# A retention-attention and SwiGLU kernel: grouped layout, fp32 row loads on the hardware queues, casts and transposes on chip, warm-up matmuls

## The chip, the cores and the metric

The kernel runs on 1 core of a Trainium2 chip. The metric is device time in microseconds (us) of one execution. Engines are named as in the profile: PE (TensorE matmul), PEld (its weight loads), DVE (VectorE), ACT (ScalarE), POOL (GpSimd), SP (SyncE). SP, ACT and POOL also issue DMAs; the queue of the DMAs that one of them issues is called its ring here.

## The reference, cut to what matters

```python
# q, k, v: [4, 8, 768, 64] fp32; lam: [8]; D[i,j] = lam**(i-j) for i >= j
for b in range(nb):                                  # sequential over blocks
    intra = einsum(einsum(qb, kb) * Dmask, vb)
    inter = einsum(qb * lam_pow, kv_state)
    out[:, :, sl] = intra + inter
    kv_state = lam_block * kv_state + einsum(kb * rev_pow, vb)
x = out.transpose(0, 2, 1, 3).reshape(3072, 512)
y = (silu(x @ w_gate) * (x @ w_val)) @ w_out         # d_ff = 1536, y: [3072, 512] fp32
```

Both kernels use blocks of 128 tokens and bf16 matmuls. A token tile of the second half ("FFN") is 512 tokens: 12 gate/value pairs of eight 128x512 matmuls, then four output groups of twelve.

## The kernel before

It walks batch by batch and two heads at a time. Loads and stores, which the argument is about:

```python
# q, k: fp32 in memory, cast to bf16 by the software queue; v: fp32, hardware queue
for h2 in range(2):
    nc.gpsimd.dma_start(out=q_nat[:, :, h2, :], in_=q_5d[b, hp, h2])   # 128-byte rows land
    nc.gpsimd.dma_start(out=k_nat[:, :, h2, :], in_=k_5d[b, hp, h2])
    nc.sync.dma_start(out=v_raw[:, :, h2, :], in_=v_5d[b, hp, h2])     # 256-byte rows
...
nc.gpsimd.dma_start(out=wg_sb, in_=moe_w_gate.rearrange("(c p) f -> p c f", p=128))  # whole weights
nc.gpsimd.dma_start(out=wv_sb, in_=moe_w_val.rearrange("(c p) f -> p c f", p=128))
...
nc.tensor.transpose(tpq[:, blk, :], q_nat[:, blk, :, :], identity)     # all transposes on PE
...
nc.scalar.copy(out=osb, in_=op)
nc.sync.dma_start(out=out[t0:t0 + TSUB, :], in_=osb)    # a store: 128 rows of 2,048 bytes
```

## Time and profile before

| | before |
|---|---|
| time, median of 4 runs | 298.97 us |
| profiled span | 295.9 us |
| first FFN gate on ACT | 56.2 us |
| period of FFN tiles 1 to 4 | 40.1, 42.2, 41.4, 39.2 us |
| last matmul to the end | 3.6 us |

The tile rows of this and later tables are read from the instruction records: a tile starts where ACT begins the first silu of that tile.

The first lines of the page of before: span, and busy tenths in 40 slices of 7.4 us (PEclk is the clock that PE was granted, in tenths of full speed); then the packets and the chain of waits that ended last.

```profile
span 295.9 us, 4660 instructions
PE   0233614999999999999999999999999999999995
PEclk9999999999999999999999999999999999999999
DMA  9999999999999110990001000100100000001012
DMA packets 81383, 23.90 MB, mean 81 GB/s; under 512 B 75729, under 2 KB 77265, under 8 KB 81361
PE 82%; DMA 13%; POOL 1%; DVE 1%; issue 1%; ACT 0%; SPq 0%; ACTq 0%; DVEq 0%; POOLq 0%
```

The first seven slices (52 us) are an opening in which PE is mostly idle and DMA is full. From the eighth slice on PE is busy in nine tenths of every slice but the last, and its clock is full.

The DMA issues of the same page: tiles, queue, count, size, median us from issue to landing.

```profile
v_raw<-in_v_dram SPq DMA_DIRECT2D x32, 192.0 KB, 9.4
out_dram<-osb SPq DMA_DIRECT2D x24, 256.0 KB, 2.0
wg_sb<-in_moe_w_gate_dram POOLq DMA_DIRECT2D x1, 1536.0 KB, 17.1
wv_sb<-in_moe_w_val_dram POOLq DMA_DIRECT2D x1, 1536.0 KB, 24.5
```

A store of 256 KB lands in 2.0 us. In the packet records each store ends in sixteen 4-byte packets, one for each DMA engine that took part.

### The profile page before, as it was taken

The page shows a single profiled execution, that of the slowest core. Times are in us where ns is not written, and L with a number is a line of the kernel's source. Part 1 is how long each engine was busy: PE and PEld are TensorE (multiplying, and loading weights), DVE is VectorE, ACT ScalarE, POOL GpSimd, SP SyncE. Part 2 cuts the span into 40 slices and gives each one's busy share as a digit, 9 for nine tenths or more (in the row PEclk, how much of TensorE's full clock was granted, in tenths as well). Part 3 has the DMA queues.
Part 4 walks back from the last instruction along what each step waited for, and adds up shares of the span by engine and source line. Part 5 has one row for each costly group of instructions (what it writes and reads, how often), then busy time and mean ns, then how long its engine had stood idle before and what let it go on. Part 6 is the DMA issues. An engine that isn't in the chain of part 4 may idle for free.

```text
span 295.9 us, 4660 instructions
## 1 busy us (share of the span) xinstructions
PE 256.3 (87%) x1824; PEld 119.3 (40%) x1824; DVE 127.2 (43%) x296; ACT 96.6 (33%) x232; POOL 57.0 (19%) x78
## 2 busy tenths in 40 slices
PE   0233614999999999999999999999999999999995
PEld 0122302446444444464444445544444444444442
DVE  1662525477654533934453444345344433222200
ACT  3411201536342422263333224524322332222321
POOL 9765015453156000840000000000000000000000
PEclk9999999999999999999999999999999999999999
DMA  9999999999999110990001000100100000001012
GB/s 153 169 169 189 209 189 157 172 182 194 168 128 115 37 39 35 73 124 35 2 35 38 34 5 35 39 0 35 38 15 23 35 35 8 29 37 38 35 72 106
DMA packets 81383, 23.90 MB, mean 81 GB/s; under 512 B 75729, under 2 KB 77265, under 8 KB 81361
## 3 DMA queue, kind: packets, MB, share of 16 engines
q0 software_dynamic: 52816, 11.02, 41.8%
q1 hardware_dynamic: 28544, 12.59, 19.9%
q8 instruction: 14, 0.23, 0.3%
q14 instruction: 9, 0.07, 0.1%
HBM read 28.32 MB, written 6.29 MB: 117 GB/s over the span
## 4 chain that ended last, share of the span: by engine, by line
PE 82%; DMA 13%; POOL 1%; DVE 1%; issue 1%; ACT 0%; SPq 0%; ACTq 0%; DVEq 0%; POOLq 0%
PE gp L255 24%; PE vp L261 22%; PE ffn_op L272 22%; DMA v_raw<-in_v_dram 8%; PE op L225 3%; DMA q_nat<-in_q_dram 3%; PE sp L196 3%; PE op L217 3%; DMA k_nat<-in_k_dram 2%; PE tpq L171 2%; PE tpk L177 1%; PE up L232 1%; DVE ssb L204 1%; PE sp L198 1%; DVE v_s L163 0%
## 5 line engine op out<-in xcount | busy, mean ns | idle before, releaser
L263 DVE TENSOR_TENSOR h_sb<-sil,vp 128x512 bf16<-128x512 bf16 x72 | 49.5, 687 | 83.7 <-PE vp L261 81.1
L272 PE MATMUL ffn_op<-wo_sb,h_sb 128*128 128x512 bf16 x288 | 65.4, 379 | 0.2
L258 ACT ACTIVATE sil<-gp 128x512 bf16<-128x512 f32 x72 | 43.0, 598 | 60.6 <-PE gp L255 60.2
L204 DVE TENSOR_TENSOR ssb<-sp,maskp_all 128x512 bf16<-128x512 f32 x48 | 33.0, 686 | 32.5 <-PE sp L198 32.5
L261 PEld LDWEIGHTS <-wv_sb 128*128 128x128 bf16 x288 | 28.0, 98 | 35.0 <-issue 3.1
L272 PEld LDWEIGHTS <-h_sb 128*128 128x128 bf16 x288 | 27.7, 98 | 31.9 <-issue 0.2
L99 POOL DMA_DIRECT2D k_nat<-in_k_dram x32 | 26.4, 830 | 52.6 <-PE up L234 24.6
L275 ACT COPY osb<-ffn_op 128x512 f32<-128x512 f32 x24 | 14.1, 586 | 62.7 <-PE ffn_op L272 62.7
L255 PEld LDWEIGHTS <-wg_sb 128*128 128x128 bf16 x288 | 23.5, 98 | 22.9 <-issue 0.3
L98 POOL DMA_DIRECT2D q_nat<-in_q_dram x32 | 26.6, 833 | 18.8 <-DMA wg_sb<-in_moe_w_gate_dram 7.3
L255 PE MATMUL gp<-xT_285,wg_sb 128*128 128x512 bf16 x72 | 28.1, 390 | 0.0
L255 PE MATMUL gp<-xT_286,wg_sb 128*128 128x512 bf16 x72 | 27.6, 383 | 0.0
L255 PE MATMUL gp<-xT_287,wg_sb 128*128 128x512 bf16 x72 | 27.6, 383 | 0.0
L255 PE MATMUL gp<-xT_288,wg_sb 128*128 128x512 bf16 x72 | 27.6, 383 | 0.0
L261 PE MATMUL vp<-xT_285,wv_sb 128*128 128x512 bf16 x72 | 27.5, 382 | 0.0
L261 PE MATMUL vp<-xT_286,wv_sb 128*128 128x512 bf16 x72 | 27.5, 382 | 0.0
L261 PE MATMUL vp<-xT_287,wv_sb 128*128 128x512 bf16 x72 | 27.3, 379 | 0.0
L261 PE MATMUL vp<-xT_288,wv_sb 128*128 128x512 bf16 x72 | 27.3, 379 | 0.0
L171 PE MATMUL tpq<-identity,q_nat 128*128 128x128 bf16 x96 | 9.2, 240 | 20.1 <-DMA q_nat<-in_q_dram 20.1
L225 PE MATMUL op<-ssb,v_s 128*64 128x128 bf16 x96 | 15.0, 241 | 12.4 <-DVE ssb L204 12.4
L178 ACT COPY kT<-tpk 128x768 bf16<-128x768 bf16 x16 | 12.8, 799 | 23.2 <-PE tpk L177 23.0
L198 PE MATMUL sp<-qT,kT 64*128 64x128 bf16 x96 | 16.4, 237 | 0.0
(90 smaller groups left out, 264.2 us busy)
## 6 DMA issues: line engine op xcount, KB each, us to landing
v_raw<-in_v_dram SPq DMA_DIRECT2D x32, 192.0 KB, 9.4
out_dram<-osb SPq DMA_DIRECT2D x24, 256.0 KB, 2.0
q_nat<-in_q_dram POOLq DMA_DIRECT2D x32, 96.0 KB, 9.5
k_nat<-in_k_dram POOLq DMA_DIRECT2D x32, 96.0 KB, 9.7
wg_sb<-in_moe_w_gate_dram POOLq DMA_DIRECT2D x1, 1536.0 KB, 17.1
wv_sb<-in_moe_w_val_dram POOLq DMA_DIRECT2D x1, 1536.0 KB, 24.5
wo_sb<-in_moe_w_out_dram POOLq DMA_DIRECT2D x1, 1536.0 KB, 18.5
lam_bcast<-in_lam_dram POOLq DMA_DIRECT2D x1, 4.0 KB, 4.1
```

What stands on the lines that cost most here:

```text
L98: nc.gpsimd.dma_start(out=q_nat[:, :, h2, :], in_=q_5d[b, hp, h2])
L99: nc.gpsimd.dma_start(out=k_nat[:, :, h2, :], in_=k_5d[b, hp, h2])
L171: nc.tensor.transpose(tpq[:, blk, :], q_nat[:, blk, :, :], identity)
L198: nc.tensor.matmul(sp[:, 1, cs], st["kT"][64:128, bs], st["qT"][64:128, bs], start=True, stop=True)
L204: nc.vector.tensor_tensor(out=ssb, in0=sp_ap, in1=mp_ap, op=ALU.mult)
L225: nc.tensor.matmul(op[0:64, :], st["v_s"][:, blk, 0, :], ssb[:, 0, ci, :], start=False, stop=True)
L255: nc.tensor.matmul(gp, wg_sb[:, mc, fs], xT[mc][:, ts], start=(mc == 0), stop=(mc == MCHUNKS - 1))
L258: nc.scalar.activation(sil, gp, AF.Silu)
L261: nc.tensor.matmul(vp, wv_sb[:, mc, fs], xT[mc][:, ts], start=(mc == 0), stop=(mc == MCHUNKS - 1))
L263: nc.vector.tensor_tensor(out=h_sb[:, fc, :], in0=sil, in1=vp, op=ALU.mult)
L272: nc.tensor.matmul(op, h_sb[:, fc, sub * TSUB:(sub + 1) * TSUB], wo_sb[:, fc, :], start=(fc == 0), stop=(fc == FCHUNKS - 1))
L275: nc.scalar.copy(out=osb, in_=op)
```

## The change

The kernel was rewritten so that PE gets work early and attention uses the array better. A group is one block of 128 tokens of two batches, with all 8 heads; there are 12 groups. Tokens 2m and 2m+1 share a partition, so that a loaded row of q, k or v is 512 contiguous bytes. Scores, values and state updates run as 64x64 quadrants of the array, four at a time. Weights come in pieces, in order of use. Groups 0 to 3 are transposed on PE, 4 to 11 by DMA. The core of it, with cuts marked:

```diff
+    def load_fp32(g, eng, src, what, b2):          # one half: 64 partitions x 8 heads x 512 bytes
+        eng.dma_start(out=st[(what, g)][b2 * M:b2 * M + M],
+                      in_=gsrc(src, g, b2, 0, [[S * D, H], [1, 2 * D]]))
+    halves = (nc.sync, nc.scalar)                  # opening: one half on each ring
+    ...
+    def w_piece(c0, c1):                           # gate and value weights for chunks c0 to c1
+        nc.gpsimd.dma_start(out=wg_sb[:, :, cs], in_=wg_d[:, :, cs])
+        nc.gpsimd.dma_start(out=wv_sb[:, :, cs], in_=wv_d[:, :, cs])
+    ...
+    def cast_scaled(g):                            # groups 4 to 11
+        nc.scalar.copy(out=t[:, 0]..., in_=st[("kraw", g)]...)
+        nc.vector.tensor_tensor(out=t[:, 1]..., in0=st[("qraw", g)]..., in1=bap(qd, ...), op=ALU.mult)
+        nc.sync.dma_start(out=tt..., in_=t..., transpose=True)
+    ...
+    nc.tensor.matmul(sp[(c, h2)][b2 * M:b2 * M + M, n:n + BLK],       # one quadrant
+                     tt[dp, 0, s, hp, b2 * M:b2 * M + M], tt[dp, 1, :, hp, b2 * M:b2 * M + M], ...)
+    ...
+    eng.dma_start(out=bass.AP(tensor=out.tensor, offset=out.offset + row * DM + c0,
+                              ap=[[DM, 2], [2 * DM, M], [1, c1 - c0]]),   # 2 x 64 rows
+                  in_=osb[:, c0:c1])
-    nc.sync.dma_start(out=out[t0:t0 + TSUB, :], in_=osb)
+    warm_up(16) ... warm_up(10)                    # matmuls on zeros in the opening
```

The store follows from the layout: partitions 0 to 63 hold the even tokens, 64 to 127 the odd ones, so the memory side of a store has the dimensions 2, 64 and 512.

## The prediction

> **What bounds the kernel now.** The span is 295.9 us; runs take 299.5, so 3.5 us lie outside it. In the chain of waits PE is 82%, DMA 13%. The slices show two stages:
>
> 1. Opening, 0 to 52 us: PE 10 to 40% busy, the DMA rows full. 81,383 packets carry 23.9 MB, 75,729 of them under 512 B: q and k come by software queue as 128-byte rows, v as 256-byte rows. Median 9.5 us to land, wg 17, wv 24. In the chain v_raw, q_nat and k_nat hold 13% (39 us).
> 2. From 57 us PE is 9 tenths busy. In the timeline a gate/value pair of eight 128x512 matmuls takes 1.74 us start to start, an output of twelve 2.6 us: 72 x 1.74 + 24 x 2.6 = 188 us, which no layout changes. The attention block between two pairs costs 0.84 us; 48 make 40 us, 192 transposes come on top. The tail after the last matmul is 3.5 us.
>
> **What the change does.**
> - Removes the 128-byte rows: q, k, v come as 512-byte fp32 rows on the SP and ACT queues. Bytes read stay at 28 MB, packets fall to about 50,000. PE starts on the first 1 MB (k, q), FFN tile 0 before all weights, which come in pieces in order of use.
> - Adds ACT/DVE casts (128x1024, estimated 1.1 to 1.3 us from v_s 128x768 at 0.95 and kT at 0.80), v scaling on POOL (estimated 2.3 us, from the Trainium skill, "GPSIMD Engine Reference", section 3.1, tensor_tensor 4,497 ns at [128, 2048]; the trace of before has none), state copies on POOL, DMA transposes for groups 4 to 11.
> - Moves attention to 64x64 quadrants: 32 score, 8 state, 32 value, 32 update matmuls per group. In the trace a concurrent pair goes every 65 to 80 ns; I estimate a quad at 80 to 100 ns, a group at 3.1 us: 12 groups, 37 us.
> - Writes output as 2 x 64 x 512. The Trainium skill, "DMA: Bandwidth & Descriptors", section "Why a DMA increments its semaphore by 16 and not by 1", says the slowest dim sets the number of DMA engines: here 2, not 16. A 2,048-byte packet takes 78 ns in the trace, so 64 per engine are 5 us, where the last five outputs come every 2.6 us: a backlog, a tail of 12 to 14 us in place of 3.5.
>
> **Sum.** Opening until the steady loop of tile 0 (third gate/value pair) 33 us, held by POOL's order (state copies before weight pieces) and the first transpose-mask chain; rest of tile 0 28; tiles 1 to 4 37.8 each (20.9 + 10.4 + 2 x 3.1 + small stalls); tile 5 31; last outputs 10.4; tail 12. Span 265, with some chance of a short tail: time 265 us, range 250 to 281. Faster by over 2%: 0.95; within 2%: 0.04; slower: 0.01. Most of the gain is the opening.
>
> **What would show it.** PE above 9 tenths from slice 6 or 7 on; the first full-width gate matmul near 33 us; a tile period near 38 us; a group's 104 matmuls taking 3 us; out_dram landing in 5 us or more, not 2.0, and over 8 us between last matmul and end.
>
> **What would make it wrong.** Output writes over 16 engines (10 us better). Quadrants that don't run together: a group at 5 us (20 us worse). Weight pieces or ACT's own DMA issues stalling tile 0 (10 us worse). DMA transposes landing late, stalling every tile. An opening under 25 us.

The marked cut takes out a time for one store packet that stands in no trace. The packets meant are those of 2,048 bytes: they take 86 ns in the trace of before (median) and 84 ns in that of after, so 64 of them are 5.4 to 5.5 us.

## The result, and the profile after

The changed kernel is correct and slower: 321.29 us median of 4 runs, against 298.97 us. The ratio is 1.0756, with a 95% interval of 1.0708 to 1.0804. A ratio here is the mean time of one kernel's fast runs over that of the other's of the same rounds, so it isn't quite the ratio of the two medians. ("Slow" on one core only means over 1.5% above the fastest run of the same kernel.)

The same lines of the page of after; a slice is 8.0 us.

```profile
span 320.5 us, 5135 instructions
PE   6187879689606979997619996808999999999400
PEclk9669959959855997999958999976999999999955
DMA  7996999999999962749670998990940101011111
DMA packets 67064, 34.40 MB, mean 107 GB/s; under 512 B 20322, under 2 KB 64098, under 8 KB 67042
PE 31%; DMA 25%; SPq 6%; ACT 1%; issue 1%; DVE 1%; ACTq 1%; POOL 0%
DMA qkt<-qk 18%; PE bank L378 12%; PE bank L368 9%; PE bank L361 8%; DMA v<-in_v_dram 7%; SPq L90 6%; PE bank L278 1%; ACTq L386 1%; ACT osb L385 1%; DVE ssb L285 1%; ACT sil L365 1%; DVE h L371 0%; SPq L205 0%; PE bank L310 0%; PE bank L300 0%
```

The opening is short: PE is busy from the third slice on, 16 us in (some of it warm-up). But three holes follow in the PE row, at 88, 160 and 208 us, the granted clock falls to 5 to 7 tenths in or just after each, and the last slices have almost no PE work. The chain names what PE waited for: `qkt<-qk`, the DMA transposes, 18% of the span, and then loads of v (7%) and SP's own issuing of row loads (6%). None of the three is in e1's chain to more than 4%, where the stores are spread.

PE's waits in after (engine, line, releaser; us in total, times, longest), then some of PE's instructions in order of time around the first hole (start, us, what, idle time before it and its releaser). L278 are the scores, which read the transposed `qkt`; L239 the transposes on PE; L361 and L368 gate and value.

```profile
PE bank L278 <- DMA qkt<-qk: 32.0, 4, 10.2
PE bank L239 <- ACT qk L223: 8.6, 1, 8.6
```

```profile
82.05 1.03 PE L368 MATMUL bank<-xt,wv_sb 128*128 128x512 bf16 x4
...
88.02 0.73 PE L330 MATMUL bank<-v_s,qk 64*64 64x64 bf16 x32
98.37 1.07 PE L278 MATMUL bank<-qkt 64*64 64x128 bf16 x32 [9.62 <-DMA qkt<-qk]
...
101.05 1.91 PE L368 MATMUL bank<-xt,wv_sb 128*128 128x512 bf16 x4
```

PE stands still for 9.62 us before the scores of group 5. (This hole is hardly the stores' doing, as e1 shows below.) The four matmuls that took 1.03 us before it take 1.91 us after it. The Trainium skill, "TensorE: Matmul & The Clock Gate", Part 1, says that PE goes to half of its clock after an idle window of about 3.4 us. This trace agrees: the granted clock of the stretch from 68 to 122 us is 0.78.

The end of the same trace, ACT and its queue:

```profile
297.55 0.58 ACT L385 COPY osb<-bank 128x512 f32<-128x512 f32 x1 [2.00 <-PE bank L378]
298.17 2.03 ACTq L386 DMA_DIRECT2D out_dram<-osb  x1
300.30 0.37 ACT L385 COPY osb<-bank 128x256 f32<-128x256 f32 x1 [2.16 <-PE bank L378]
300.70 6.09 ACTq L386 DMA_DIRECT2D out_dram<-osb  x1
```

Issuing the last store on ACT takes 6.09 us, where a usual issue takes 0.52. The span ends at 320.5 us, 20.4 us after the last matmul. In the packet records a store ends in two 4-byte packets, and its 2,048-byte packets take 84 ns each: two DMA engines carry it, 64 packets each, 5.4 us of their time.

Where the time went, by stage (us, one profiled run each). Rows e1 to e11 are the experiments below.

| kernel | first gate | tile 0 | tile 1 | tile 2 | tile 3 | tile 4 | last matmul | tail | span |
|---|---|---|---|---|---|---|---|---|---|
| before | 56.2 | 31.5 | 40.1 | 42.2 | 41.4 | 39.2 | 292.3 | 3.6 | 295.9 |
| after | 32.1 | 36.3 | 58.3 | 48.7 | 50.7 | 33.8 | 300.1 | 20.4 | 320.5 |
| e1 | 30.9 | 36.6 | 54.4 | 35.4 | 36.7 | 34.3 | 268.0 | 4.8 | 272.7 |
| e2 | 33.1 | 38.0 | 46.4 | 33.7 | 37.4 | 34.7 | 263.5 | 20.4 | 283.8 |
| e3 | 31.3 | 37.2 | 43.7 | 38.0 | 38.0 | 35.2 | 263.0 | 4.8 | 267.8 |
| e4 | 55.8 | 32.2 | 40.1 | 42.2 | 41.4 | 39.2 | 292.6 | 19.9 | 312.5 |
| e6 | 32.2 | 37.6 | 40.9 | 35.5 | 35.4 | 34.3 | 255.6 | 4.9 | 260.5 |
| e9 | 31.8 | 35.2 | 48.6 | 36.0 | 35.4 | 34.3 | 260.8 | 4.8 | 265.6 |
| e11 | 29.8 | 37.5 | 41.3 | 35.4 | 35.4 | 34.3 | 253.2 | 4.9 | 258.1 |

(In after and in e1 to e3 and e6 to e11, "first gate" is the first full-width one: four half-width pairs come earlier, so tile 0 has ten full pairs.)

### The profile page after: what moved, and what is told of

It reads as the page before. It is cut to its first block, busy times and chain, and to the rows that moved or that the text cites. A ratio compares the mean times of both kernels' runs of the same rounds, so it can differ in the third digit from the quotient of the medians.

```text
span 320.5 us, 5135 instructions
## 1 busy us (share of the span) xinstructions
PE 237.4 (74%) x2112; PEld 117.4 (37%) x2138; DVE 105.6 (33%) x185; ACT 89.7 (28%) x149; POOL 66.9 (21%) x106
## 2 busy tenths in 40 slices
DMA packets 67064, 34.40 MB, mean 107 GB/s; under 512 B 20322, under 2 KB 64098, under 8 KB 67042
## 4 chain that ended last, share of the span: by engine, by line
PE 31%; DMA 25%; SPq 6%; ACT 1%; issue 1%; DVE 1%; ACTq 1%; POOL 0%
DMA qkt<-qk 18%; PE bank L378 12%; PE bank L368 9%; PE bank L361 8%; DMA v<-in_v_dram 7%; SPq L90 6%; PE bank L278 1%; ACTq L386 1%; ACT osb L385 1%; DVE ssb L285 1%; ACT sil L365 1%; DVE h L371 0%; SPq L205 0%; PE bank L310 0%; PE bank L300 0%
## 5 line engine op out<-in xcount | busy, mean ns | idle before, releaser
L371 DVE TENSOR_TENSOR h<-sil,bank 128x512 bf16<-128x512 bf16 (+1 forms) x74 | 49.6, 672 | 123.7 <-PE bank L368 61.7
L361 PE MATMUL bank<-xt,wg_sb 128*128 128x512 bf16 (+1 forms) x277 | 77.9, 395 | 5.9 <-DMA wg_sb<-in_moe_w_gate_dram 2.7
L368 PE MATMUL bank<-xt,wv_sb 128*128 128x512 bf16 (+1 forms) x295 | 79.8, 396 | 1.4 <-DMA wv_sb<-in_moe_w_val_dram 1.2
L365 ACT ACTIVATE sil<-bank 128x512 bf16<-128x512 f32 (+1 forms) x74 | 43.1, 585 | 107.4 <-PE bank L361 95.1
L378 PE MATMUL bank<-wo_sb,h 128*128 128x512 bf16 x283 | 66.2, 383 | 5.0 <-DVE ssb L285 4.7
L368 PEld LDWEIGHTS <-wv_sb 128*128 128x128 bf16 x296 | 30.1, 103 | 40.0 <-issue 7.8
L378 PEld LDWEIGHTS <-h 128*128 128x128 bf16 x288 | 28.7, 100 | 40.9 <-issue 8.6
L361 PEld LDWEIGHTS <-wg_sb 128*128 128x128 bf16 x296 | 28.8, 101 | 38.9 <-issue 7.1
L285 DVE TENSOR_TENSOR ssb<-bank,mask 128x512 bf16<-128x512 f32 x48 | 31.4, 683 | 32.8 <-PE bank L278 32.8
L344 POOL CAST kvz<-kvf 64x256 bf16<-64x256 f32 x40 | 15.8, 396 | 113.6 <-DVE kvf L341 110.3
L278 PE MATMUL bank<-qkt 64*64 64x128 bf16 x384 | 9.4, 249 | 33.8 <-DMA qkt<-qk 32.0
L385 ACT COPY osb<-bank 128x512 f32<-128x512 f32 (+1 forms) x24 | 13.8, 576 | 65.0 <-PE bank L378 65.0
L189 POOL TENSOR_TENSOR v_s<-v,rev 128x1024 bf16<-128x1024 f32 x12 | 23.1, 1925 | 30.8 <-DMA v<-in_v_dram 30.6
L278 PEld LDWEIGHTS <-qkt 64*64 64x64 bf16 x384 | 7.4, 125 | 35.4 <-DMA qkt<-qk 32.5
L239 PE MATMUL bank<-ident,qk 128*128 128x128 bf16 x64 | 5.2, 243 | 9.9 <-ACT qk L223 8.6
L239 PEld LDWEIGHTS <-qk 128*128 128x128 bf16 x64 | 4.5, 110 | 11.1 <-ACT qk L223 9.1
```

The costliest lines, as they stand in the source:

```text
L189: eng.tensor_tensor(out=st[("vs", g)][:, h0:h1], in0=st[("v", g)][:, h0:h1].rearrange("p h (s d) -> p h s d", s=2), in1=bap(rev, [[2, h1 - ...
L278: nc.tensor.matmul(sp[(c, h2)][b2 * M:b2 * M + M, n:n + BLK], tt[dp, 0, s, hp, b2 * M:b2 * M + M], tt[dp, 1, :, hp, b2 * M:b2 * M + M], st ...
L285: nc.vector.tensor_tensor(out=ssb[:, h2, 2 * c:2 * c + 2].rearrange("p a s n -> p (a s n)"), in0=sp[(c, h2)], in1=mask[:, h2, 2 * c:2 * c ...
L344: nc.gpsimd.tensor_copy(out=kvz[b][dp, :, h2, :], in_=kvf[b][dp])
L361: nc.tensor.matmul(gp[:, 0:N], wg_sb[:, mc, fs], xt[:, mc, b0:b1].rearrange("p b n -> p (b n)"), start=(mc == 0), stop=(mc == MC - 1))
L365: nc.scalar.activation(sil[:, 0:N], gp[:, 0:N], AF.Silu)
```

## The experiments

My theory, A: stores on two DMA engines hold up what shares those engines, the DMA transposes above all. Rival B: DMA transposes are slow by themselves, or because they stand behind row loads on SP. Rival C, later: it isn't the number of engines, but the size or count of the stores.

### e1, e2, e3, e4: stores and transposes apart

e1 splits each store in two halves of 64 partitions, one of even and one of odd rows:

```diff
-            eng.dma_start(out=bass.AP(..., offset=out.offset + row * DM + c0,
-                                      ap=[[DM, 2], [2 * DM, M], [1, c1 - c0]]), in_=osb[:, c0:c1])
+            for s in range(2):
+                eng.dma_start(out=bass.AP(..., offset=out.offset + (row + s) * DM + c0,
+                                          ap=[[2 * DM, M], [1, c1 - c0]]),
+                              in_=osb[s * M:s * M + M, c0:c1])
```

> The changed kernel with one edit: each output store is split in two of 64 partitions, so that the slowest dimension is 64 and 16 DMA engines carry it, not 2. Theory A (stores on 2 DMA engines hold up everything else on those engines, the DMA transposes above all): the transposes of groups 4 to 11 land in about 5 us, PE's waits for them (32 us) fall under 5 us, the tail after the last matmul falls from 23 us to 4 us, and the time is 255 to 265 us. Rival B (the DMA transposes are slow by themselves, or because they stand behind the row loads on the SP queue): only the tail goes, about 19 us, and the time is 300 to 305 us with the waits for the transposes still there.

e2 leaves the stores and puts all transposes on PE (groups 4 and 5, in tile 1, likewise; cut here):

```diff
-                    at(6, cast_scaled, 2 * t + 4)
-                    at(11, cast_scaled, 2 * t + 5)
+                    at(6, cast_qk, 2 * t + 4)
+                    at(7, pe_transpose, 2 * t + 4)
+                    at(11, cast_qk, 2 * t + 5)      # its pe_transpose: step 1 of the next tile
```

> The changed kernel with groups 4 to 11 cast and transposed on the chip's TensorE, as groups 0 to 3 are; the stores stay on 2 DMA engines. Theory A: no wait for a DMA transpose is left, but the stores still crowd two engines, so loads may come late and the tail stays near 15 to 23 us: 272 to 285 us. Rival B (transposes alone are to blame): the same 272 to 285 us, and then e1 gives 300 us or more. The two runs together tell them apart.

e3 is both edits.

> Both edits: stores on 16 DMA engines and all transposes on TensorE. Theory A: near e1, within 3 us, 255 to 265 us, since with free engines the DMA transposes cost PE nothing. Rival B: at least 30 us faster than e1.

e4 is the kernel before with the store's shape alone (rows land in the wrong order):

```diff
-            nc.sync.dma_start(out=out[t0:t0 + TSUB, :], in_=osb)
+            nc.sync.dma_start(out=bass.AP(..., ap=[[DM, 2], [2 * DM, 64], [1, DM]]), in_=osb)
```

> The kernel before, with its output rows written as 2 x 64 rows (even rows, odd rows), so that 2 DMA engines carry a store; the rows land in the wrong order, a wrong result on purpose. Theory A: this part of the change alone costs the tail, as four stores of 5 us come every 2.5 us at the end: 8 to 13 us more than before, 307 to 312 us, and little in the middle, where no DMA transpose waits. Rival B (store shape harmless apart from some latency): within 2% of before.

Measured (median us, ratio to before of the same rounds):

| | DMA transposes | PE transposes |
|---|---|---|
| stores on 2 engines | 321.29 (1.0756, the changed kernel) | 286.06 (0.9599, e2) |
| stores on 16 engines | 273.64 (0.9193, e1) | 268.58 (0.9014, e3) |

e4: 314.41 us, ratio 1.0555.

Splitting the stores alone takes 47.7 us off (321.29 to 273.64). Moving the transposes alone takes 35.2 us off, both together 52.7. The two don't add: stores on two engines cost 17.5 us where there are no DMA transposes, and 47.7 us where there are. The 17.5 us are nearly all tail: e2's tail is 20.4 us and e3's 4.8. e4 says the same on the other kernel: the periods of its tiles 1 to 4 are those of before to 0.1 us, its tail is 19.9 us and not 3.6, and the time is 16.3 us longer. The other 30 us arise only where DMA transposes and stores meet.

Of e1's expectations, the tail and the direction came true. The time missed the expected 255 to 265 us, because tile 1 still takes 54.4 us, and one wait for a transpose is left:

```profile
PE bank L278 <- DMA qkt<-qk: 8.3, 1, 8.3
```

That wait is again the one for group 5, the hole shown at 88 us in after: 9.62 us there, 8.27 here. In neither run does a store packet start while that transpose moves, so the stores' part in this wait is at most the 1.35 us between the two (e9 takes it up). What the split removed are the other three of after's four waits, 22.4 of the 32.0 us: 2.29 for group 6, 9.98 for group 8, 10.16 for group 10. The last two in after's chain (start, us, what), from the issue of the transpose to the scores:

```profile
148.17 18.98 DMA qkt<-qk
167.19 1.07 PE bank L278 x24
...
198.72 18.71 DMA qkt<-qk
217.48 1.07 PE bank L278 x29
```

The DMA issues of e1 (tiles, queue, count, size, median us to landing); the trace of after gives no landing for its stores and transposes.

```profile
out_dram<-osb ACTq DMA_DIRECT2D x46, 128.0 KB, 2.4
qkt<-qk SPq DMA_TRANSPOSE x8, 5.5
```

e2 came out just above its range; e3 beat e1 by 5 us, not 3, and lay above its 255 to 265; e4 lost 16.3 us, not 8 to 13. In all three the sign was as A said, and in e1 rival B's 300 us did not come.

How a few stores on two engines hold a transpose that all engines carry is seen in the packet records. One DMA transpose is 2,048 packets of 256 bytes. In group 7 of after they take 22 ns each on average, 45 us in all, within 2.6 us: some 17 at a time, so I estimate that all 16 engines carry it. The table gives the time from its first packet to the start of the packet at a quarter, half, three quarters, seven eighths and all of it, and the store packets (2,048 bytes) that started meanwhile, for six of the transposes. (Not shown of after: groups 9 and 11 took 7.8 and 9.5 us beside 122 and 131 store packets, groups 4 and 5 took 3.0 and 4.4 us beside none.)

| transpose of group | 25% | 50% | 75% | 87.5% | all | store packets |
|---|---|---|---|---|---|---|
| after, 7 | 0.7 | 1.3 | 1.9 | 2.2 | 2.6 us | 3 |
| after, 6 | 0.7 | 1.3 | 5.2 | 6.7 | 10.7 us | 166 |
| after, 8 | 6.8 | 9.7 | 12.7 | 14.0 | 14.8 us | 256 |
| after, 10 | 6.8 | 9.7 | 12.8 | 14.1 | 15.0 us | 256 |
| e1, 8 | 1.7 | 2.4 | 2.8 | 3.0 | 3.4 us | 55 |
| e1, 10 | 1.2 | 1.9 | 2.3 | 2.6 | 3.4 us | 78 |

If the stores held up only the transpose's share on their own two engines, 2 of 16, then seven eighths of the packets would be through in about 2.2 us. In groups 8 and 10 that takes 14 us: the whole transpose is held, and not a share of it. That it must keep its engines in step, and so moves at the pace of the two busy ones, is my reading of these rows; the records don't name the engine of a packet. Row loads run meanwhile too (235 and 259 packets of 512 bytes in groups 8 and 10 of after, 35 and 26 in e1), and the rows alone don't part them from the stores. But in e2 loads meet the same stores without DMA transposes, and tiles 2 and 3 take 33.7 and 37.4 us, against 48.7 and 50.7.

### e5, e12: four and eight engines

The same single store, with other row orders (wrong results), so that the slowest dimension is 4 or 8:

```diff
-                                      ap=[[DM, 2], [2 * DM, M], [1, c1 - c0]]),
+                                      ap=[[DM, 4], [4 * DM, BLK // 4], [1, c1 - c0]]),   # e12: 8, 8, 8
```

> The changed kernel with its output rows written as 4 x 32 rows (a wrong row order on purpose), so that 4 DMA engines carry a store, not 2; still one store for each tile, DMA transposes as they were. Theory A (the number of engines decides): a store takes half of its 5.4 us, which is about the 2.6 us between the last outputs, so the tail falls from 20 us to about 7 us, PE's waits for DMA transposes fall to between those of after (32 us) and e1 (8 us), and the time is 280 to 292 us, between 321 and 274. Rival C (what helped in e1 was to issue two smaller stores, not the engines): within 5 us of 321.

> As e5, with the output rows written as 8 x 16 rows (wrong order on purpose), so that 8 DMA engines carry one store; still one store for each tile. e5 was unclear (one run at 285.5 us, three near 297). Theory A (the number of engines decides): a store is an eighth of the rows on each engine, 16 packets, about 1.4 us, so the tail is about 5 to 6 us and a DMA transpose beside a store loses 1 to 3 us: 274 to 282 us. Rival C (the count of stores or their half partitions decided in e1): 295 us or more.

e5 gave 285.52 us in its one fast run; the other three took 296 to 298 us. It has no interval: the fast run lies in A's range, the others lie between A's range and rival C's, and I can't say why it has two levels. e12 gave 272.88 us (all six runs 270.3 to 275.4, two of them slow), ratio 0.9103 with 0.9052 to 0.9154. This is just below A's range and no slower than e1, with one store for each output group as in the changed kernel. So rival C falls: the number of engines decides, and here eight are enough. The profiled runs go the same way. Their tails are 20.4 us with 2 engines, 10.3 with 4, 5.4 with 8 and 4.8 with 16, and tiles 2 and 3 together take 99.4, 89.2, 69.8 and 72.1 us (those of e5 and e12 were slow).

### e6, e9: why tile 1 stays long

In e1 the cast for group 5's transpose was done at 82.4 us. SP was then still issuing row loads of group 6, and came to the transpose at 85.5. The chain of waits of e1 in this stretch (start, us, what):

```profile
85.51 9.80 DMA qkt<-qk
95.31 0.04 issue
95.35 1.07 PE bank L278 x32
```

e6 is e1 with the transposes of groups 4 and 5 on PE. e9 is e1 with group 6's loads moved behind that transpose:

```diff
+                    at(3, load_group, 6)            # t == 1, after cast_scaled(5)
-                    at(0, load_group, 2 * t + 4)
+                    if t > 1:
+                        at(0, load_group, 2 * t + 4)
```

> Stores on 16 engines as in e1, and TensorE transposes for groups 4 and 5 alone, whose DMA transposes e1 still waited for in tile 1; groups 6 to 11 keep their DMA transposes. Theory A: tile 1 takes 44 us as in e3, tiles 2 to 4 take 35 to 37 us as in e1, so 262 to 267 us, the fastest so far. Rival B (DMA transposes cost something in every tile even with free engines): no better than e3, 268 us or more.

> e1 with one change of order on SP: in tile 1 the six row loads of group 6 are issued after group 5's DMA transpose, not before it. In e1 that transpose was issued 3 us after its cast was done and landed 9.8 us later, at 95.3 us, where PE waited 8.3 us for it. If the order on SP is the second cause (beside the stores), tile 1 falls from 54 us to 44 to 48 us and the time from 274 to 263 to 268 us. If the transpose is slow in any order, the time stays within 2 us of e1.

e6: 262.04 us, ratio 0.8796, at the low end of what I expected: tile 1 falls from 54.4 to 40.9 us (44 expected), and tiles 2 and 3 take 35.5 and 35.4. PE waits for none of e6's DMA transposes, where transposes on PE make a tile 38.0 us (e3). e9: 270.11 us (median of four runs, one of them slow), ratio 0.9019, above the expected 263 to 268. The 8.3 us wait is gone, the longest for a transpose is 2.6 us, and group 5's transpose runs in 2.7 us from its first packet. But tile 1 falls only to 48.6 us, just outside what I expected. So the order on SP, a part of rival B, makes about 6 of the 13.5 us by which e1's tile 1 exceeds e6's; the rest of tile 1 in e9 I haven't separated.

### e7, e8: warm-up and rings

```diff
-    warm_up(16)          # e7: both warm-ups out of e3
-    warm_up(10)
-    halves = (nc.sync, nc.scalar)
+    halves = (nc.sync, nc.sync)      # e8: all of group 0 from SP, on e3
```

> e3 without both warm-up runs of matmuls on zeros. If the warm-up matters, the first group's transposes, scores and values run at half clock for longer and the time rises by 2 to 4 us over e3 (270.5 to 273). If not (PE idles 8 us between the first warm-up and the first transpose anyway, and the opening waits for DMA), within 1 us of e3.

> e3 with both halves of group 0's k, q, v issued from SP, none from ACT. The two halves share the same DMA engines, so only issue time is lost, 0.65 us for each of three more issues on SP: the first transposes start 0.5 to 1.5 us later and the time is 268.5 to 270.5 us. If separate rings double the rate of loading, the opening would be 3 us longer or more: 271.5 us or more.

e7: 268.86 us, ratio 0.9025, within 0.3 us of e3. In after the first warm-up ends at 6.2 us, and PE then idles 8.6 us until the first cast is done (the second wait listed above), long enough to lose the clock again by the page on the clock gate cited above: the sixteen transposes that follow take 1.89 us, the same sixteen of the next group 1.07. The second warm-up, from 18.98 to 22.10 us, only fills the wait for the masking of the scores, which ends at 20.73, and runs past it. e8: 267.39 us, ratio 0.8969. If anything that is 1 us faster than e3; the intervals overlap (e3: 0.8981 to 0.9046, e8: 0.8941 to 0.8998). It isn't the loss that I expected. The Trainium skill, "DMA: Bandwidth & Descriptors", in its rules for kernel authors, says of two transfers to disjoint partition halves "Don't bother", since both use the same DMA engines. This run agrees as far as it goes: the second ring brought nothing, 267.39 us without it against 268.58 with it. (One transfer of all 128 partitions wasn't tried.) So the warm-up, which the change is named for, and the second ring show no gain here.

### e10, e11: a version that beats both

e10 is e6 with weight pieces of four chunks where they were two; e11 adds e8's single ring.

```diff
-    w_piece(4, 6)
+    w_piece(4, 8)
...
-    w_piece(6, 8)
-    w_piece(8, 10)
-    w_piece(10, 12)
+    w_piece(8, 12)
```

> e6 with the gate and value weights loaded in pieces of four chunks (4 to 8, 8 to 12), 1,024-byte destination rows, in place of pieces of two with 512-byte rows. In the traces a 512-byte row that is cast took 59 ns and a 1,024-byte one 97 ns, so I estimate about 20% faster weights. If tile 0 (37 us, of which 10 pairs and two groups need 25) is held by the weights, it falls by 2 to 4 us, and the time to 258 to 260 us. If not, within 1 us of e6, or worse because larger pieces land later.

> e10 and all of the first group's loads from SP, as in e8. Expected within 2 us of e10; if e8's lead of 1 us over e3 was real, 1 us faster.

e10: 261.18 us, ratio 0.8756. Tile 0 didn't get shorter (38.1 us), so larger pieces don't lift what holds it; the time stayed within 1 us of e6, the other outcome that I had named. e11: 259.74 us, ratio 0.8693 (0.8652 to 0.8733), correct, and 39 us faster than before. Its page:

```profile
span 258.1 us, 5250 instructions
PE   8596569587898999999999999999999999999992
PEclk9769889999799999999999999999999999999998
```

From slice 14 (84 us) on PE is busy as it was in before, and the clock is full. What is left lies in tiles 0 and 1.

## Why the prediction was wrong

The prediction said 265 us, range 250 to 281, and 0.95 for faster by over 2%. It was 321 us, 7.6% slower. Its sum beside the trace:

| term | predicted | measured in after |
|---|---|---|
| opening, to the third gate/value pair | 33 | 31.3 (first full-width gate matmul) |
| opening and tile 0 | 61 | 68.4 |
| tiles 1 to 4 | 4 x 37.8 = 151 | 58.3 + 48.7 + 50.7 + 33.8 = 191.5 |
| tile 5 and last outputs | 41.4 | 40.2 |
| tail | 12 | 20.4 |

- **The step that failed**: "tiles 1 to 4 37.8 each (20.9 + 10.4 + 2 x 3.1 + small stalls)". The stalls weren't small; this term is 40 us short. The prediction had both facts in hand: two engines for a store, 5 us for each; and groups 4 to 11 by DMA transpose. It put the first into the tail only and named the second as a risk, "DMA transposes landing late, stalling every tile", without a size. It never asked what else uses the engines that the stores occupy. e1 to e3 show that the product of the two, and not either alone, is the 30 us (tiles 1 to 4 take 191.5 us in after, 160.8 in e1). A further 13.5 us of tile 1 (e1's 54.4 against e6's 40.9) is the first two DMA transposes, partly by order on SP (e9). The two come to more than the 40 us, since the work itself was less than I took it for (attention, below): e6's tiles 1 to 4 take 146.1 us.
- **Mis-sized: the tail**, 12 to 14 us said, 20.4 measured. The last five stores are issued from 290.40 us on, the last matmul ends at 300.1, and five times 5.4 us on the same two engines alone lead to 317.4; start and completion add about 3. The prediction's own numbers (five stores of 5 us) gave about 15 before start and completion, and I rounded down. e4 shows that the tail by itself costs 16.3 us.
- **Mis-sized: the rest of tile 0**, 28 us said, 37.1 measured (68.4 less 31.3). What holds it stays open.
- **Right: two engines for a store.** The Trainium skill, "DMA: Bandwidth & Descriptors", section "Why a DMA increments its semaphore by 16 and not by 1", has the rule; the trace shows two final packets and 5.4 us of packet time. With the store spread, e1 lost 47.7 us. "Output writes over 16 engines (10 us better)" was far too small a guess.
- **Right: the opening.** 33 us said, 31.3 measured for the first full-width gate matmul; in before that matmul starts at 52.6.
- **Too high: attention.** A group was put at 3.1 us. In e3, where nothing waits, the 104 matmuls of a group run from 124.02 to 125.89 us, 1.87 us in all; the four equal blocks of before take 4 x 0.84 = 3.4. The quadrants do run together. PE work for tiles 1 to 4 was thus less than I took it for, and the stalls larger still.

These lines of e3, PE in order of time, are that group: state, values, update, and the next group's scores.

```profile
124.02 0.61 PE L300 MATMUL bank<-qkt,kvz 128*128 128x128 bf16 x8
124.56 0.64 PE L310 MATMUL bank<-ssb,v_s 64*64 64x128 bf16 x32
125.03 0.45 PE L330 MATMUL bank<-v_s,qk 64*64 64x64 bf16 x32
125.30 0.65 PE L278 MATMUL bank<-qkt 64*64 64x128 bf16 x32
```

- **Too high: POOL.** Its scaling was estimated at 2.3 us from the Trainium skill, "GPSIMD Engine Reference", section 3.1; it takes 1.93 us on average in after. This didn't matter.
- **Too low: packets.** 50,000 said, 67,064 counted: I left out the 16,384 packets of the DMA transposes.

What stays open: why e5 has two levels, what holds tile 0 at 35 to 38 us where its matmuls need about 23 (ten pairs of 1.74, two groups of 1.87, the transposes of two groups at 1.06 each), and what part of tile 1 in e9 is which wait.

## What to carry to other kernels

Look at the slowest dimension of both sides of every DMA, stores too: two rows of 64 is not the same as 128 rows, and here a store split in two cut 48 us. Where a few DMA engines are crowded, ask which other transfer uses them too: here the DMA transposes took 14.8 to 15.0 us where they took 2.6, and PE paid twice, once in waiting (9.98 and 10.16 us) and once in a lower clock after the wait. A cost that a prediction has found at one place, such as the tail, must be carried through every stage in which the same resource is used.

## What the Trainium skill lacked or had wrong

- "DMA: Bandwidth & Descriptors", rules for kernel authors, says that a transpose next to ordinary DMAs needs nothing. That speaks of correct data, and all results with stores in the right order were correct. It doesn't say what it costs: a 512 KB DMA transpose ran in 2.6 us with almost nothing beside it and in 14.8 to 15.0 us beside stores on two engines, slow in every quarter (6.8, 2.9, 3.0 and 2.1 us in group 8).
- The same page, "Why a DMA increments its semaphore by 16 and not by 1", has the rule for the number of engines; the runs agree (2, 4, 8 or 16 final packets for a store) and add its price: tails of 20.4, 10.3, 5.4 and 4.8 us for 2, 4, 8 and 16 engines.
- "Perfetto Trace Analysis", "DMA Instruction — HWDGE (DVE, Sync)", says of what an issue on the issuing engine consists, and that descriptors may not fit in their buffer, but not how long an issue becomes behind a backlog: the last store's issue took ACT 6.09 us, against 0.52 for others, and the issue of group 8's transpose took SP 11.24 us, against 1.32 for group 11's. That their queues were full is my reading.
- "GPSIMD Engine Reference", section 3.1, gives 4,497 ns for a tensor_tensor add at N = 2048 in fp32; half of that is 2,249 ns (an estimate for N = 1024), and the runs show means of 1,925 ns (after) to 2,058 ns (e1) for a multiply at 128x1024 with fp32 in and bf16 out, as far as the profile's POOL spans, which are rough, can say.
